# A larger planned gap between a batch's folds and its sequence products

## The chip, the cores and the metric

The kernel runs on one core of a Trainium2 chip, in fp32. Its time is the device time of one execution in microseconds (us). Five runs of the kernel before gave a median of 827.72 us (826.7 to 829.09). The names of the engines are those of the profile: PE is TensorE (matrix products), DVE is VectorE, ACT is ScalarE, POOL is GpSimd (which also issues the gathers), and SP issues most of the plain transfers.

## The reference

```python
# lightning attention: q, k, v (4, 8, 768, 64), lam (8,)
intra = einsum('bhij,bhjd->bhid', einsum('bhic,bhjc->bhij', qb, kb) * Dmask, vb)
inter = einsum('bhid,bhde->bhie', qb * lam_pow, kv_state)
out[:, :, sl] = intra + inter
kv_state = lam_block * kv_state + einsum('bhsd,bhse->bhde', kb * rev_pow, vb)
# bridge: x[b, s, h*64 + d] = out[b, h, s, d]          (4, 768, 512)
# FNet block, w_ch1 (512, 2048), w_ch2 (2048, 512)
mixed = real(fft(fft(x, axis=1), axis=2))
u = x + mixed
un = (u - mean(u)) / sqrt(var(u) + 1e-6)
result = u + maximum(un @ w_ch1, 0) @ w_ch2
```

Each of the four batches is independent of the others, apart from the weights that all share.

## The kernel before, in words

**A batch's front.** Attention goes through a batch in six chunks of 128 rows (`NC` = 6). `attn_in` loads k, q and v of a chunk (L263), turns k and q with PE (L274, L279), copies them out with ACT (`kT` L276, `qT` L281) and scales q with DVE (L285). `attn_out` makes the scores (16 products L298, which take the two halves of PE's rows in turn), multiplies them by the decay on DVE (`sc`, two of L302), updates the state (L315 on PE, L317 or L320 on DVE), adds the state's part and the scores' part (L328, L332), copies the result out (L335) and turns it (L348) into x. Parts of x go to DRAM (`xa`, `xb`; L363 to L367), since the Fourier mixing needs rows in mirrored order: POOL gathers these (`mirror_a`, L439 and L445; `mirror_b`, L452).

`fft_ln` then mixes. By the symmetry of a real Fourier transform, `fold_a` and `fold_b` first add and subtract mirrored rows and columns on DVE (L426 to L430 and L470 to L484). The sequence products (L516, against the table `cs`, in two pieces of 128 and 65 rows) and the width products (L529 to L534, against `dt`) follow. DVE combines them (L596 to L609), normalises (statistics L546 and L547, the root on POOL L550 and L551, `un` L564), and the result is kept for the MLP: of the first four groups of 256 rows it is turned with PE (L569), of the other eight it is turned in blocks by DVE (L574) and stored by SP (L578, L584).

**The MLP.** The twelve groups are named `(b, g)`. The first four, `PLAIN`, are multiplied plainly by `mlp`: for each of 16 blocks of the hidden width, four products with `w1` (L633, a "group" of four below) and a relu on ACT or DVE (L641, L639); then for each of two tiles of 128 rows, products with `w2` (L647), the addition of u (L654 and L655 in a first half, L658 and L659 in the last part, into `y`), and the store (L620 by SP, or L622, a scatter by POOL). Three of the four are done in two halves of the hidden width. The other eight, `LATE`, are done after all fronts, in pairs, with fewer block products by a Strassen-Winograd form (L720, L767). The weights come in double precision and are converted on the way by ACT and DVE (`load_weights`, L209 to L225).

**What sets the order.** The functions are generators. They issue instructions and then yield a number, the time on PE or DVE that the planner takes as due for what came since the last yield. `weave(lead, other, ratio)` runs the `lead`, and after each of its yields draws from `other` until that one's sum reaches the lead's sum times `ratio`. `beside` derives the ratio from planned lengths. A yield that follows no instruction of its own is a request for so much other work at that place. In the last two of these weaves the fronts of batches 1 (rest), 2 and 3 run against the plain products: in the first, the products lead, the fronts get `t_rest * t_half / t_back` units; in the second, the fronts lead. A further scheduler then fixes the order of instructions on each engine from the program as built, taking account of their data and of the buffers that they take over; some instructions are pinned in program order.

The lengths that concern the change: `t_chunk` = 7.3, `t_front` = 6 x 7.3 + 13.0 + 7.0 + 5.7 + 3 x 2.4 = 76.7, `t_mlp` = 54.4, `t_half` = 81.6, `t_back` = 167.6, `t_rest` = 3 x 76.7 - 5 x 7.3 = 193.6. `LEADS` = (0,), so `b - 1 in LEADS` holds for batch 1 only, and L508 gives 12.0 for batch 1 and 9.0 for batches 2 and 3. Batch 0 takes another branch.

**Buffers.** x tiles come from a pool of 12; a gathered x (L452) takes over the buffer of an older one, such as the u of a plain tile whose last reader is L659. PE's results go to five buffers (`pa`, fronts) and three (`pm`, products).

Of the kernel before, what the change touches and what calls it, by code (L numbers as in the profile page):

```python
# [76 lines left out]
def kernel(  # L77
# [15 lines left out]
    NC = S // C  # L93
# [161 lines left out]
    LEADS = (0,)  # L255
# [200 lines left out]
    def fold_a(b):  # L456
        for a, n in enumerate(BLK):
            yield from fold_x(b, a, n, 1, eo[b][a][1][0:n, 1, 0:DM], xn_[b, HC + a][0:n])

    def fold_b(b, sets):  # L460

        tt = nc.vector.tensor_tensor
        for a, n in enumerate(BLK):
            yield from fold_x(b, a, n, 0, xs[b, a][0:n], xs[b, HC + a][0:n])
            e, o = eo[b][a]
            nc.scalar.copy(e[0:n, :, HM:HM + 1], e[0:n, :, DM - 1:DM])

            am, bm = e[0:n, :, W:2 * W], o[0:n, :, W:2 * W]
            lo, hi = e[0:n, 0, 0:HM + 1], e[0:n, 1, 0:HM + 1]
            tt(am[:, 0, 0:HM + 1], lo, hi, op=ALU.add)  # L470
            tt(am[:, 1, 0:HM + 1], lo, hi, op=ALU.subtract)
            yield 0.8

            lo, hi = am[:, :, 0:QM], am[:, :, HM:QM:-1]
            tt(e[0:n, :, 0:QM], lo, hi, op=ALU.add)
            tt(e[0:n, :, QM:HM], lo, hi, op=ALU.subtract)
            yield 0.8
            lo, hi = o[0:n, 0, 1:HM], o[0:n, 1, 1:HM]
            tt(bm[:, 0, 1:HM], lo, hi, op=ALU.subtract)
            tt(bm[:, 1, 1:HM], lo, hi, op=ALU.add)  # L480
            yield 0.8
            lo, hi = bm[:, :, 1:QM + 1], bm[:, :, HM - 1:QM - 1:-1]
            tt(o[0:n, :, 0:QM], lo, hi, op=ALU.subtract)
            tt(o[0:n, :, QM:HM], lo, hi, op=ALU.add)  # L484
            yield 0.8
            sets.append((e, o))
        eo.pop(b)
# [3 lines left out]
    def fft_ln(b):  # L491
# [7 lines left out]
        if b in LEADS:  # L499
            yield from fold_a(b)  # L500
            yield from fold_b(b, sets)
            yield 2.0
        else:
            yield 1.0
            run(fold_a(b))
            yield 6.0 if b - 1 in LEADS else 3.0
            run(fold_b(b, sets))
            yield 12.0 if b - 1 in LEADS else 9.0  # L508


        for i in range(5):
# [288 lines left out]
    def front(b):  # L800
        yield from attn(b)
        yield from fft_ln(b)
# [15 lines left out]
    def run(gen):  # L818
        return sum(gen)
# [12 lines left out]
    NW = 2 * KO * DFF // WP  # L832
    w = weights()
    t_chunk = 7.3
    t_front = NC * t_chunk + 13.0 + 7.0 + 5.7 + 3 * 2.4
    t_mlp = FO * 1.7 + G * 4 * 3.4

    def beside(lead, t, other, t_other):
        return weave(lead, part(other, t_other), t_other / t)

    att1, mix = attn(1), fft_ln(0)
    att0 = attn(0)
    run(part(att0, 2.7))
# [4 lines left out]

    half = [[mlp(b, g, h * FO // 2, (h + 1) * FO // 2) for b, g in PLAIN[:3]] for h in range(2)]
    fr = chain([att1, fft_ln(1)] + [front(b) for b in range(2, B)])  # L850
    t_rest, t_back = 3 * t_front - 5 * t_chunk, len(PLAIN) * t_mlp - 50.0
    t_half = 1.5 * t_mlp
# [50 lines left out]
```

## Time and profile before

| | us |
|---|---|
| median of 5 runs | 827.72 (826.7 to 829.09) |
| the profiled execution's own time | 825.68 |
| its span | 823.9 |
| PE busy in the span | 797.0 |
| end of the fronts and plain products, start of the late pairs | about 433 |

The times of instructions come from one profiled execution, which took 825.68 us; 1.8 us of it lie around the span. The granted clock of PE was 0.996 of full speed. In lists of instructions each line has the start and the duration in us, the engine, the line of the kernel, the operation with its output and inputs, and how many instructions of a kind follow each other. A bracket at the end is the idle time of the engine ahead of the instruction, and the instruction that ended it. In fp32 each matrix product appears as two records. In lists of waits the columns are the sum in us, how many times, and the longest. [...]

### The profile page before, as it was taken

The page shows a single profiled execution, that of the slowest core. Times are in us where ns is not written, and L with a number is a line of the kernel's source. Part 1 is how long each engine was busy: PE and PEld are TensorE (multiplying, and loading weights), DVE is VectorE, ACT ScalarE, POOL GpSimd, SP SyncE. Part 2 cuts the span into 40 slices and gives each one's busy share as a digit, 9 for nine tenths or more (in the row PEclk, how much of TensorE's full clock was granted, in tenths as well). Part 3 has the DMA queues.
Part 4 walks back from the last instruction along what each step waited for, and adds up shares of the span by engine and source line. Part 5 has one row for each costly group of instructions (what it writes and reads, how often), then busy time and mean ns, then how long its engine had stood idle before and what let it go on. Part 6 is the DMA issues. An engine that isn't in the chain of part 4 may idle for free.

```text
span 823.9 us, 11701 instructions
## 1 busy us (share of the span) xinstructions
PE 797.0 (97%) x4608; PEld 636.2 (77%) x4608; DVE 437.8 (53%) x1018; ACT 186.4 (23%) x448; POOL 79.9 (10%) x102
## 2 busy tenths in 40 slices
PE   6889799999999999999999999999999999999998
PEld 5777676758585857768748888888888888888886
DVE  6899779675744571345895541155313661146311
ACT  3655343324420211222102200022001210012100
POOL 3123310011010110220100000000000000000000
PEclk9999899999999999999999999999999999999999
DMA  9969443238841137530442011100111001000010
GB/s 235 251 146 272 107 154 103 77 77 217 205 117 59 64 65 141 128 122 1 115 126 79 1 53 51 52 1 0 58 46 52 0 1 39 33 33 0 1 39 25
DMA packets 126684, 68.88 MB, mean 84 GB/s; under 512 B 111150, under 2 KB 112174, under 8 KB 126630
## 3 DMA queue, kind: packets, MB, share of 16 engines
q1 hardware_dynamic: 121488, 55.67, 26.3%
q0 software_dynamic: 2112, 6.69, 2.5%
q10 hardware_dynamic: 3030, 5.78, 1.9%
q8 instruction: 36, 0.59, 0.3%
q14 instruction: 18, 0.15, 0.1%
HBM read 48.72 MB, written 19.40 MB: 83 GB/s over the span
## 4 chain that ended last, share of the span: by engine, by line
PE 81%; DVE 10%; issue 4%; DMA 2%; ACT 2%; POOL 1%; SPq 0%; POOLq 0%; ACTq 0%; DVEq 0%
PE p L767 24%; PE p L720 23%; PE pm L647 10%; PE pm L633 8%; PE pa L298 3%; PE pa L516 3%; PE pa L332 3%; PE pa L328 2%; PE pa L274 1%; PE pa L315 1%; PE pa L348 1%; PE pa L279 1%; DVE fe L426 1%; DMA x<-xb,ix 1%; DVE fo L427 1%
## 5 line engine op out<-in xcount | busy, mean ns | idle before, releaser
L633 PE MATMUL pm<-ut,w 128*128 128x256 f32 x512 | 119.9, 383 | 0.0
L647 PE MATMUL pm<-w,hr 128*128 128x512 f32 x256 | 115.8, 597 | 0.3 <-DVE w L225 0.3
L633 PEld LDWEIGHTS pm<-ut,w 128*128 128x128 f32 x512 | 94.2, 190 | 15.8 <-issue 4.1
L720 PE MATMUL p<-ur,w 128*128 128x256 f32 x384 | 93.8, 379 | 0.0
L647 PEld LDWEIGHTS pm<-w,hr 128*128 128x128 f32 x256 | 46.7, 190 | 49.7 <-issue 47.8
L720 PEld LDWEIGHTS p<-ur,w 128*128 128x128 f32 x384 | 73.0, 190 | 10.3 <-issue 0.5
L720 PE MATMUL p<-us,w1s 128*128 128x256 f32 x256 | 65.7, 379 | 0.0
L767 PE MATMUL p<-w,hs 128*128 128x256 f32 x256 | 58.0, 379 | 0.5 <-DVE y L788 0.5
L767 PE MATMUL p<-w2s,hs 128*128 128x256 f32 x256 | 57.9, 379 | 0.0
L767 PE MATMUL p<-w,ha 128*128 128x256 f32 x256 | 57.9, 379 | 0.0
L767 PEld LDWEIGHTS p<-w,hs 128*128 128x128 f32 x256 | 48.5, 190 | 7.5 <-DVE y L788 0.9
L767 PEld LDWEIGHTS p<-w2s,hs 128*128 128x128 f32 x256 | 48.6, 190 | 6.6
L767 PEld LDWEIGHTS p<-w,ha 128*128 128x128 f32 x256 | 48.6, 190 | 6.6
L720 PEld LDWEIGHTS p<-us,w1s 128*128 128x128 f32 x256 | 48.6, 190 | 6.6
L622 POOL DMA_INDIRECT out_dram<-y,ix x12 | 11.9, 988 | 401.9 <-DVE y L793 342.3
L747 ACT COPY ha<-p 128x256 f32<-128x256 f32 x32 | 11.9, 372 | 169.1 <-PE p L720 139.4
L758 DVE TENSOR_TENSOR ha<-p,ha 128x256 f32<-128x256 f32 x32 | 13.6, 424 | 45.2 <-ACT ha L757 45.2
L298 PEld LDWEIGHTS pa<-qT,kT 64*128 64x128 f32 x384 | 26.3, 194 | 13.2 <-ACT qT L281 7.1
L302 DVE TENSOR_TENSOR sc<-pa,decay 128x512 f32<-128x512 f32 x48 | 31.5, 683 | 8.8 <-PE pa L298 8.5
L332 PE MATMUL pa<-sc,v 128*64 128x128 f32 x384 | 31.6, 281 | 3.7 <-DVE sc L302 3.5
L298 PE MATMUL pa<-qT,kT 64*128 64x128 f32 x384 | 30.9, 293 | 3.3 <-ACT qT L281 3.0
L720 PE MATMUL p<-us,w 128*128 128x256 f32 x128 | 32.9, 379 | 0.0
(144 smaller groups left out, 1122.3 us busy)
## 6 DMA issues: line engine op xcount, KB each, us to landing
raw<-in_moe_w_ch_dram SPq DMA_DIRECT2D x32, 512.0 KB, 5.0
k<-in_k_dram SPq DMA_DIRECT2D x24, 256.0 KB, 5.0
q<-in_q_dram SPq DMA_DIRECT2D x24, 256.0 KB, 5.9
v<-in_v_dram SPq DMA_DIRECT2D x24, 256.0 KB, 4.4
ud<-x SPq DMA_DIRECT2D x16, 256.0 KB, 2.3
utd<-e SPq DMA_DIRECT2D x64, 64.0 KB, 2.2
u<-ud SPq DMA_DIRECT2D x16, 256.0 KB, 2.7
ur<-utd SPq DMA_DIRECT2D x6, 512.0 KB, 4.9
```

The costliest lines, as they stand in the source:

```text
L298: mm(pss[hi][:, hp, :], lhsT=kT[HD[hi], hp, :], rhs=qT[HD[hi], hp, :], start=True, stop=True)
L302: nc.vector.tensor_tensor(t, pss[hi], decay[:, hi::2, :], op=ALU.mult)
L328: mm(po[HD[hi], hp, :], lhsT=s_old[HD[hi], hp, :], rhs=qs[HD[hi], hp, :], start=(hp == 0), stop=False, skip_group_check=True)
L332: mm(po[HD[hi], hp, :], lhsT=vt[:, 2 * hp + hi, :], rhs=sc[hi][:, hp, :], start=(c == 0 and hp == 0), stop=(hp == HP - 1), skip_group_chec ...
L516: mm = nc.tensor.matmul(ps[0:m, n, :], lhsT=piece(a, i, n), rhs=cs[0:rows, a, i in (2, 3), n, :], start=(a == 0), stop=(a == 1))
L622: nc.gpsimd.indirect_dma_start(out=out.rearrange("b s d -> (b s) d"), out_offset=row_of(2 + HC * (b + 1) + T - HC), in_=y[:, :], in_offset ...
L633: nc.tensor.matmul(ps, lhsT=w1[:, c, 128 * fc:128 * fc + 128], rhs=ut[:, c, :], start=(c == 0), stop=(c == KO - 1))
L647: nc.tensor.matmul(ps, lhsT=hr[(fc - f0) // 4][:, fc % 4, 128 * i:128 * i + 128], rhs=w2[:, fc, :], start=(fc == f0), stop=(fc == f1 - 1))
L720: nc.tensor.matmul(ps, lhsT=s2.A[a][:, kt, 128 * i:128 * i + 128], rhs=U[b][:, kt, :], start=(first and kt == 0), stop=(kt == 1), skip_gro ...
L747: nc.scalar.copy(a11, two(X))
L758: V.tensor_tensor(a22, two(Z), a22, op=ADD)
L767: nc.tensor.matmul(ps, lhsT=h[a][:, s, i, :], rhs=s2.B[b][:, i, :], start=(first and i == 0), stop=(i == HF - 1), skip_group_check=True)
```

## The change

Two constants grow by 2.5. At the end of the folds of batches 2 and 3, ahead of their sequence products, the yield becomes 11.5 in place of 9.0. The planned length of a front becomes 79.2 in place of 76.7, and through it `t_rest` 201.1 in place of 193.6. What is computed, by which instructions and from which buffers' pools, stays as it is; the order of instructions on the engines changes from batch 1's mixing on.

```diff
             yield 6.0 if b - 1 in LEADS else 3.0
             run(fold_b(b, sets))
-            yield 12.0 if b - 1 in LEADS else 9.0
+            yield 12.0 if b - 1 in LEADS else 11.5
...
-    t_front = NC * t_chunk + 13.0 + 7.0 + 5.7 + 3 * 2.4
+    t_front = NC * t_chunk + 15.5 + 7.0 + 5.7 + 3 * 2.4
```

The code that turns these numbers into an order:

```python
    def beside(lead, t, other, t_other):
        return weave(lead, part(other, t_other), t_other / t)
...
    t_rest, t_back = 3 * t_front - 5 * t_chunk, len(PLAIN) * t_mlp - 50.0
    run(beside(beside(chain(half[0]), t_half, w, 0.5 * NW), t_half + 0.5 * NW, fr, t_rest * t_half / t_back))
...
    run(weave(fr, back, (t_back - t_half) / (t_rest - t_rest * t_half / t_back)))
```

## The prediction

> **What bounds the kernel now.** I read the page's busy row first, then a table of stages, then TensorE's waits in the stage that the change touches, and last the two places where the change aims. The page:
>
> ```profile
> span 823.9 us, 11701 instructions
> PE 797.0 (97%) x4608; PEld 636.2 (77%) x4608; DVE 437.8 (53%) x1018; ACT 186.4 (23%) x448; POOL 79.9 (10%) x102
> ```
>
> TensorE (PE) is the bound: 26.9 us of the span are not its busy time. The stage table (PE busy is the first figure after the stretch's length) says where these lie:
>
> ```profile
> 0.00:134.00 134.00, 116.16 (x1062) 89.90 (x1062) 111.61 (x243) 64.94 (x146) 34.56 (x45) 0.97 0.71 183
> 134.00:433.00 299.00, 294.02 (x1757) 206.43 (x1757) 183.27 (x386) 73.38 (x174) 36.55 (x48) 1.00 0.43 110
> 433.00:823.90 390.90, 386.86 (x1792) 339.86 (x1790) 142.97 (x391) 48.05 (x128) 8.75 (x9) 1.00 0.09 29
> ```
>
> In the built order of the changed program the first stage and the last hold the same instructions in the same order as before. All that the change can win lies in the middle one: 299.00 - 294.02 = 5.0 us. TensorE's waits there (in all, times, longest):
>
> ```profile
> PE pa L516 <- DVE fe L475: 2.2, 3, 1.1
> PE pa L332 <- DVE sc L302: 1.6, 1, 1.6
> PE pa L569 <- DVE un L564: 0.9, 1, 0.9
> PE pm L647 <- DVE w L225: 0.3, 1, 0.3
> ```
>
> The first row is the change's aim: the sequence products L516 of batches 2 and 3 find their fold unfinished, 1.06 + 0.19 us in batch 2 and 0.95 in batch 3. What holds the fold, in batch 2, all engines:
>
> ```profile
> 257.50 0.41 DVE L659 TENSOR_TENSOR y<-pm,x 128x256 f32<-128x256 f32 x1
> ...
> 258.19 0.94 POOL L452 DMA_INDIRECT x<-xb,ix  x1 [11.88 <-DVE y L659]
> ...
> 261.58 0.69 DVE L426 TENSOR_TENSOR fe<-x,x 128x512 f32<-128x512 f32 x1 [3.66 <-DMA x<-xb,ix]
> ...
> 265.06 0.90 PE L516 MATMUL pa<-cs,fe 128*128 128x193 f32 x4 [1.06 <-DVE fe L475]
> ```
>
> The gather L452 doesn't wait for the attention. It waits for L659, the end of a plain MLP tile, whose x buffer it takes over. So the fold is released by the products themselves.
>
> **What the Trainium skill says.** "Perfetto Trace Analysis", Identifying the Most-Contended Engine: matmul busy time misleads, and weight-load time is to be read beside it. Here that is 77%, with PE waits nearly absent after 134 us; I judge by waits. The same page, Optimization Strategy, has one find the gaps and what would end them: done above. Its Sequencer Loop lets an instruction wait in its engine's queue for its semaphores; the trace agrees, a wait of 0.56 us at L564 standing directly ahead of a score's scaling:
>
> ```profile
> 171.07 0.74 DVE L564 TENSOR_SCALAR un<-x,mv,rs 128x256 f32<-128x256 f32 x2 [0.56 <-POOL rs L551]
> 171.72 0.68 DVE L302 TENSOR_TENSOR sc<-pa,decay 128x512 f32<-128x512 f32 x1
> ```
>
> **The change part by part.** Nothing is added or removed: each engine has the same instructions. (a) The due at L508 rises 2.5 for batches 2 and 3. (b) The planned length of a front rises 2.5, 76.7 to 79.2, and counts three times, so three fronts are planned 7.5 longer while only two are, by 5. With t_rest 193.6 to 201.1 and t_half/t_back 81.6/167.6, the first weave gives the front 97.9 for 94.3 units; the last one's products per front unit fall from 86/99.3 = 0.866 to 86/103.2 = 0.833. L508 is thus worth 9 x 0.866 = 7.79 before and 11.5 x 0.833 = 9.58 after: 1.79 product units, one L633 group more (due 1.7; 8 records, 3.62/16 x 8 = 1.8 us). Everything else in the fronts gets 4% fewer products beside it. Following the built order of both programs, with durations from the trace:
>
> Batch 2, L508. Between the last L348 and the first L516 there are 17.25 us of products before, 18.98 after. But the added group comes ahead of the MLP tile that releases the gather; from the tile's end at 257.0 to L516 stand the same 16 L647 records (6.9 us), against a chain of 8.0 (gather issue 258.19, data in use 261.58, eight fold steps on DVE). The gap 1.06 stays, and the 0.19 behind it: **0**.
>
> Batch 3, L508. After the last L348 there are 8 L647 records and 32 L633 before (3.43 + 6.91) and 12 and 24 after (5.15 + 5.19): 10.34 both times. Here the gather waits for the row's own DMA, so the chain is unmoved: the 0.95 stays. **0**.
>
> What is left is the 4%, which regroups products in the attention chunks. In fp32 each matmul is two records.
>
> - Batch 1's mixing: L569 follows 5 L633 matmuls instead of 3, but a weight step (L225, 0.6) and a relu come ahead of its un. The stall of 0.94 becomes about 1.05: **+0.1**.
> - Batch 2, chunk 0. Before, 6 L647 records, L315 and 8 L647 records (6.65 us) lie between L298 and L332; the 8 move behind L332, leaving 3.2. The second sc ends at 171.72 + 0.68 = 172.4 (queued behind L564's wait above), while PE comes to L332 at 175.30 - 3.45 = 171.85. With the 0.1 from a sc's end to its L332, a new wait of 0.65. But the width products of batch 1's last two parts now have one L633 matmul between them, not seven, so DVE gets that mixing earlier; adding up its new queue from 154.6 (with the wait for rs, 1.2 us after L547, as in the trace) I get 172.05 for the sc's end, a wait of 0.3. I take the middle: **+0.5** (0 to 1.7, if two DVE steps more come ahead).
> - Chunk 1. The 16 L298 run in turn between the two row halves, which they don't before (1.16 us for 16 elsewhere, 1.63 here): **-0.37**. L298 to L332 goes from 4.7 to 3.4 us of cover, against 2.0 of DVE work: 0.
> - Chunk 2: L332 is no longer cut by an L633 (re-entry after each switch, 0.43): **-0.43**.
> - Chunk 3. L279 to L298 falls from 3.0 to 0.87 us, while qT needs a copy of 0.59 behind another on ACT, and the row halves fall out of turn (0.37): **+0.65** (0.4 to 1.2).
> - Batch 3, chunk 0. The third wait row:
>
> ```profile
> 298.94 0.43 PE L332 MATMUL pa<-sc,v 128*64 128x128 f32 x2 [1.57 <-DVE sc L302]
> 299.31 0.55 PE L274 MATMUL pa<-ident,k 128*128 128x128 f32 x3
> ```
>
>
> L302 is late because DVE is full with batch 2's last mixing (back to back from 293.65 to 299.8). The front runs one L633 group earlier and the cover grows from 3.2 to 4.9 us; PE reaches L332 at the same time, and the second sc has moved behind five other DVE steps, to end near 299.2. The wait stays, about 1.8, but L332 isn't cut by L274: **-0.4** (-1.7, if DVE's backlog starts earlier too, to +0.3).
> - Chunks 1 to 5 of batch 3: covers change by under 2 us and stay above need; 0. The group that the front overtakes there lands in a row of products without a wait: 0.
>
> These last two are hidden by the products queued on PE; with that cover gone each would cost up to the group's 1.7. On SP's queue some weight loads change places with loads of k, q and v. The tightest of these (batch 2, chunk 3, issued at 197.83, transposed at 206.14) takes 5.0 us to land, so 3.3 are spare, and it moves ahead of a weight load: 0. POOL's gathers and scatters keep their order: 0.
>
> Sum: 0.1 + 0.5 - 0.37 - 0.43 + 0.65 - 0.4 = **+0.05 us**. The profiled execution took 825.68 (span 823.9 and 1.8 around it), 2.0 below the median of the runs, 827.72. I carry the difference over: 827.8. The ends of the terms (0, 0, -0.37, -0.43, +0.4, -1.7, and 0.2, 1.7, 0, 0, 1.2, 0.3) put this at -2.1 to +3.4; not all fall alike, so the forecast's own range is -1.2 to +1.6 us, 826.5 to 829.3.
>
> **Rivals.**
> - *The fold waits close.* If the gather's wait is set by issue time rather than by the tile, or the added group slips behind the tile, 1.06 + 0.19 + 0.95 = 2.2 us go. For it: it is what the due does by its name. Against: the releaser above, L659, and equal work in batch 3. Time 827.72 - 2.2 = 825.5; with the 1.57 as well, 823.9.
> - *DVE's queue becomes what PE waits for, in batch 2's first chunks (slower).* The place is L332 of chunk 0 and L298 of chunks 1 and 3. Between the end of L298 and the end of the second sc DVE has 4.1 us of work before (168.28 to 172.40); the cover left is 3.2. My forecast has about 4.0. Should one weight step (L224, 1.1) and one width step (L600, 0.7) come ahead of that sc too, the wait grows by 1.8; with chunk 3 at its upper end, 0.55 more: 0.05 + 1.8 + 0.55 = +2.4, 830.1. It decides (over 0.2%) from about 5.6 us of DVE work there. For it: L564's wait in this very queue. Against: the earlier width products just named.
> - *The change doesn't do what it says*: a longer due that buys no cover at all. That is in my forecast, batch 3's equal 10.34 us.
>
> **How the numbers follow.** 0.2% of 827.72 is 1.66 us, about what a measurement of this kernel tells from no change: faster is below 826.06, slower above 829.38. The forecast has 0.45, DVE's queue 0.30, the closing waits 0.25. The first lies almost all within 0.2%, the others outside. The 8-in-10 range takes in most of both: 825.6 (nearly the whole 2.2) to 830.6 (the slower rival and 0.5 more).
>
> **What would show it.** Right: the L516 rows of batches 2 and 3 keep waits of about 1.1 and 0.95 on L475; the gather before batch 2's L516 still names L659; a new wait L332 on L302 of 0.2 to 0.8 near 172; the wait at the next batch's first chunk stays at 1.5 to 2. Wrong: no L516 wait left (first rival), or waits of L332 and L298 that sum to 4 or more in the middle stage (second). It would also be wrong if the last stage changed in length: then the cause would be outside all this.

## The result, and the profile after

The kernel after took 827.79 us (median of 41 runs, 825.96 to 830.25) and the kernel before 826.47 (median of 78 runs, 824.8 to 830.64). The ratio is 1.0017, with a 95% interval of 1.0011 to 1.0024: 1.4 us slower, which is within the 0.2% named in the prediction. The five runs that the prediction started from had a higher median, 827.72. The profiled execution took 828.27 us.

The busy row of the page after:

```profile
span 826.5 us, 11699 instructions
PE 798.4 (97%) x4608; PEld 637.4 (77%) x4608; DVE 438.8 (53%) x1018; ACT 186.8 (23%) x448; POOL 79.5 (10%) x102
```

PE is still the bound. The middle row of the stage table, with the same borders as before:

```profile
134.00:433.00 299.00, 292.66 (x1754) 205.69 (x1753) 184.73 (x388) 73.69 (x175) 37.03 (x48) 1.00 0.42 110
```

In the middle stage PE is now idle for 299.00 - 292.66 = 6.3 us; it was 5.0. PE's waits there:

```profile
PE pa L516 <- DVE fe L475: 2.9, 4, 1.0
PE pa L332 <- DVE sc L302: 1.9, 2, 1.3
PE pa L569 <- DVE un L564: 0.9, 1, 0.9
PE pm L647 <- DVE w L225: 0.4, 1, 0.4
PE pm L633 <- DVE hr L639: 0.2, 1, 0.2
```

The row that the change aims at, L516, has grown from 2.2 us in three waits to 2.9 in four, the row L332 has a second wait, and there is a new row for L633. Where these are, in the list of PE's instructions:

```profile
172.48 0.43 PE L332 MATMUL pa<-sc,v 128*64 128x128 f32 x2
173.58 1.09 PE L332 MATMUL pa<-sc,v 128*64 128x128 f32 x14 [0.67 <-DVE sc L302]
...
266.22 0.90 PE L516 MATMUL pa<-cs,fe 128*128 128x193 f32 x4 [0.97 <-DVE fe L475]
...
300.35 1.09 PE L332 MATMUL pa<-sc,v 128*64 128x128 f32 x14 [1.27 <-DVE sc L302]
...
371.96 0.59 PE L516 MATMUL pa<-cs,fe 128*128 128x193 f32 x2 [0.79 <-DVE fe L475]
...
376.86 2.23 PE L516 MATMUL pa<-cs,fe 65*128 65x193 f32 x12 [0.96 <-DVE fe L475]
...
403.78 3.72 PE L633 MATMUL pm<-ut,w 128*128 128x256 f32 x16 [0.19 <-DVE hr L639]
```

Batch 2's fold wait (0.97) and batch 3's second one (0.96) are still there. New are 0.67 in batch 2's first chunk, 0.79 at batch 3's first sequence product, and 0.19 behind the front. One wait is shorter, that in batch 3's first chunk: 1.27 after 1.57.

Waits alone don't give the sum, since a row of products that is cut in two also costs. So I compared both traces at the same work: the start of the same instruction of a front in both, corrected for the plain products that have gone ahead of it in one program and not in the other (0.43 us for each L633 product of two records, 0.86 for each L647). A difference that appears between two such marks arose between them. The comparison begins at batch 1's first L516, up to which the order is the same in both programs. It stands at 135.26 us before and 136.13 after. That 0.87 us is no effect of the change.

| place | predicted | measured, us |
|---|---|---|
| batch 1's mixing, L569 | +0.1 | -0.06 |
| batch 2, chunk 0 | +0.5 | +0.91 |
| chunk 1 | -0.37 | -0.68 |
| chunk 2 | -0.43 | -0.57 |
| chunk 3, with 4 | +0.65 | +0.75 |
| batch 2's fold | 0 | -0.10 |
| batch 3, chunk 0 | -0.4 | -0.26 |
| batch 3, chunk 1 | 0 | -0.20 |
| batch 3's fold | 0 | **+0.97** |
| behind the fronts, to the late pairs | 0 | **+0.53** |
| not placed, ahead of the late pairs | | +0.07 |
| late pairs | 0 | +0.33 |
| sum from batch 1's first L516 | +0.05 | +1.69 |

The timing says +1.4 (0.9 to 2.0). Of the 1.69 in the traces, about 1.2 is idle time of PE (5.91 after 4.72 up to the late pairs), and 0.33 belongs to the last stage. The prediction's terms for the mixing and the chunks sum to 0.05; these rows measure -0.11, chunk 1 of batch 3 among them. The loss is in the two bold rows, which the prediction had at nothing.

**Batch 3's fold.** The gather of the last rows waits for the last DMA write `xb` (L367). ACT's issue of that write, and POOL's gathers, in the kernel after (ACTq is ACT's queue of issues):

```profile
361.55 0.33 ACTq L367 DMA_DIRECT2D xb<-xn  x1
```

```profile
360.26 0.99 POOL L445 DMA_INDIRECT x<-xa,ix  x1 [0.30 <-issue]
...
365.30 0.94 POOL L452 DMA_INDIRECT x<-xb,ix  x1 [4.05 <-DMA xb<-xn]
```

The same in the kernel before:

```profile
362.56 0.33 ACTq L367 DMA_DIRECT2D xb<-xn  x1
```

```profile
359.55 0.99 POOL L445 DMA_INDIRECT x<-xa,ix  x1 [0.30 <-issue]
...
365.39 0.94 POOL L452 DMA_INDIRECT x<-xb,ix  x1 [4.84 <-DMA xb<-xn]
```

The write is issued 1.0 us earlier after the change, and PE runs earlier with it, but the gather starts at nearly the same time: from issue to gather is 3.75 us in place of 2.83. What stands differently is the third gather from `xa` (L445): 3.0 us ahead of the write before, 1.3 us after. The fold isn't earlier, PE is, and this shows as the new wait of 0.79. An experiment below tests the gather as the cause.

**Behind the fronts.** The longer planned front leaves one more group of L633 products to run after the last width products. Before:

```profile
399.90 5.45 PE L633 MATMUL pm<-ut,w 128*128 128x256 f32 x24
```

These 24 records of L633 take 5.29 us up to the first L647 at 405.19. After, 32 take from 399.87 to 407.34, 7.47 us; at 0.22 us a record, 7.05 would do. The relu that PE waits for (`hr`, L639) is on DVE, behind the mixing (L600):

```profile
402.71 0.69 DVE L600 TENSOR_TENSOR x<-x,ds 128x512 f32<-128x512 f32 x1
403.31 0.42 DVE L639 TENSOR_SCALAR hr<-pm 128x256 f32<-128x256 f32 x1
```

Of the difference of 0.42, 0.19 is the bracket above and the rest a slower restart of the row; another 0.1 comes at the change to L647.

**The last stage.** The first eight records of L720 take 2.20 us after, 1.89 before; behind them both traces keep step. In the kernel after the fifth of them starts at 435.99, 0.15 us behind the end of L659 (435.84), the last step of the last plain tile. In two versions below (due of 13 for batch 3) PE waits for L659 by name at this record, and starts it the same 0.15 behind. In the kernel before, the fifth record starts at 433.52, ahead of L659's end (433.75), so it doesn't need this tile there. The +0.33 looks like a short wait for a buffer that this tile frees (0.08 us idle, and a slower restart), but the trace after doesn't name the releaser.

### The profile page after: what moved, and what is told of

Its sections match the earlier page's. It is cut to its first block, busy times and chain, and to the rows that moved or that the text cites. A ratio compares the mean times of both kernels' runs of the same rounds, so it can differ in the third digit from the quotient of the medians.

```text
span 826.5 us, 11699 instructions
## 1 busy us (share of the span) xinstructions
PE 798.4 (97%) x4608; PEld 637.4 (77%) x4608; DVE 438.8 (53%) x1018; ACT 186.8 (23%) x448; POOL 79.5 (10%) x102
## 4 chain that ended last, share of the span: by engine, by line
PE 77%; DVE 12%; issue 4%; DMA 3%; ACT 2%; POOL 1%; POOLq 0%; DVEq 0%; ACTq 0%; SPq 0%
PE p L767 23%; PE p L720 23%; PE pm L647 9%; PE pm L633 6%; PE pa L332 3%; PE pa L516 3%; PE pa L298 3%; PE pa L328 2%; DVE stt L546 1%; DMA raw<-in_moe_w_ch_dram 1%; PE pa L274 1%; DVE un L564 1%; PE pa L315 1%; PE pa L348 1%; DVE sc L302 1%
## 5 line engine op out<-in xcount | busy, mean ns | idle before, releaser
L633 PE MATMUL pm<-ut,w 128*128 128x256 f32 x512 | 120.2, 383 | 0.2 <-DVE hr L639 0.2
L647 PE MATMUL pm<-w,hr 128*128 128x512 f32 x256 | 115.5, 597 | 0.4 <-DVE w L225 0.4
L633 PEld LDWEIGHTS pm<-ut,w 128*128 128x128 f32 x512 | 94.1, 190 | 16.2 <-issue 4.1
L720 PE MATMUL p<-ur,w 128*128 128x256 f32 x384 | 94.1, 379 | 0.1
L647 PEld LDWEIGHTS pm<-w,hr 128*128 128x128 f32 x256 | 46.8, 190 | 50.8 <-issue 48.7
L720 PEld LDWEIGHTS p<-ur,w 128*128 128x128 f32 x384 | 72.9, 190 | 10.7 <-issue 0.5
L720 PE MATMUL p<-us,w1s 128*128 128x256 f32 x256 | 65.7, 379 | 0.0
L720 PEld LDWEIGHTS p<-us,w1s 128*128 128x128 f32 x256 | 48.6, 190 | 6.6
L298 PEld LDWEIGHTS pa<-qT,kT 64*128 64x128 f32 x384 | 26.8, 198 | 13.0 <-ACT qT L281 6.3
L302 DVE TENSOR_TENSOR sc<-pa,decay 128x512 f32<-128x512 f32 x48 | 31.3, 681 | 10.4 <-PE pa L298 10.2
L332 PE MATMUL pa<-sc,v 128*64 128x128 f32 x384 | 32.2, 286 | 3.4 <-DVE sc L302 3.4
L298 PE MATMUL pa<-qT,kT 64*128 64x128 f32 x384 | 31.5, 297 | 2.9 <-ACT qT L281 2.6
L720 PE MATMUL p<-us,w 128*128 128x256 f32 x128 | 32.9, 379 | 0.0
```

The lines of the kernel that those rows point to most:

```text
L298: mm(pss[hi][:, hp, :], lhsT=kT[HD[hi], hp, :], rhs=qT[HD[hi], hp, :], start=True, stop=True)
L302: nc.vector.tensor_tensor(t, pss[hi], decay[:, hi::2, :], op=ALU.mult)
L332: mm(po[HD[hi], hp, :], lhsT=vt[:, 2 * hp + hi, :], rhs=sc[hi][:, hp, :], start=(c == 0 and hp == 0), stop=(hp == HP - 1), skip_group_chec ...
L633: nc.tensor.matmul(ps, lhsT=w1[:, c, 128 * fc:128 * fc + 128], rhs=ut[:, c, :], start=(c == 0), stop=(c == KO - 1))
L647: nc.tensor.matmul(ps, lhsT=hr[(fc - f0) // 4][:, fc % 4, 128 * i:128 * i + 128], rhs=w2[:, fc, :], start=(fc == f0), stop=(fc == f1 - 1))
L720: nc.tensor.matmul(ps, lhsT=s2.A[a][:, kt, 128 * i:128 * i + 128], rhs=U[b][:, kt, :], start=(first and kt == 0), stop=(kt == 1), skip_gro ...
```

## The experiments

All compute the reference's outputs in full. This table has all of them. "From the first L516" is the time from batch 1's first L516 to the first product of the late pairs (L720), "from L720" the time from there to the span's end, each from the one profiled execution. The times are medians, and each version has the runs of the kernel before that were taken beside it. A ratio is not the quotient of the two medians; where runs scatter the two differ (due alone with `b12` later: 0.9978 by the medians; due 15 with `b12` later: 1.0062).

| kernel | time (before), us | ratio, 95% interval | from the first L516 | from L720 |
|---|---|---|---|---|
| before | | | 297.39 | 391.25 |
| after | 827.79 (826.47) | 1.0017, 1.0011 to 1.0024 | 298.75 | 391.58 |
| due alone | 826.26 (826.74) | 0.9987, 0.9974 to 1.0 | 295.77 | 393.21 |
| planned front alone | 829.45 (826.74) | 1.0032, 1.0022 to 1.0043 | 299.41 | 391.58 |
| due 15 for batch 2, 11.5 for batch 3 | 834.62 (826.74) | 1.0087, 1.0053 to 1.012 | 302.33 (low clock) | 399.39 (low clock) |
| after, third gather last | 826.89 (826.74) | 1.0009, 0.9996 to 1.0022 | 298.17 | 391.56 |
| due alone, `b12` later | 824.85 (826.71) | 0.9991, 0.9978 to 1.0005 | 294.91 | 392.17 |
| before, `b12` later | 827.28 (826.71) | 1.0004, 0.9991 to 1.0018 | 297.52 | 391.25 |
| due 15 and 11.5, `b12` later | 831.83 (826.71) | 1.0079, 1.0051 to 1.0108 | 295.65 | 397.72 (low clock) |
| due 9 for batch 2, 13 for batch 3, `b12` later | 828.36 (826.71) | 1.0033, 1.002 to 1.0046 | 297.78 | 393.68 |
| after, cover of chunk 0 back | 827.23 (826.69) | 1.0011, 0.9998 to 1.0025 | 296.82 | 391.25 |
| due alone, `b12` later, one store by POOL | 824.46 (826.69) | 0.9978, 0.9965 to 0.9992 | 295.02 | 391.35 |
| due 13 for batch 3, the same two edits | 827.47 (826.69) | 1.0011, 1.0003 to 1.0019 | 297.76 | 392.27 |
| before, the same two edits | 826.15 (827.46) | 0.9985, 0.9975 to 0.9996 | 297.74 | 390.82 |

### Each half of the change alone

My theory was that the loss is the thinner interleaving that the longer planned front brings. The rival: the longer due by itself holds back the end of the fronts.

```diff
-            yield 12.0 if b - 1 in LEADS else 9.0
+            yield 12.0 if b - 1 in LEADS else 11.5
```

> Only the due of 11.5 (L508), the planned front left at 76.7. Built order: batch 2's chunks as before; the first sequence product of batch 2 as before (its wait of 1.06 us stays); 31 plain products instead of 20 between batch 3's last turn (L348) and its first L516, so the wait there (0.95 before, 0.79 + 0.96 with the whole change) goes. Theory A, only the covers count: 0.95 gone and the cut at batch 3's first L332 (about 0.3), so about -1.2 us, ratio 0.9985, no wait of TensorE at L720. Theory B, DVE's tail is full: batch 3's mixing ends 3.4 us later, the weights' combination (L697) and L710 to L713 end up to 3 us later, and TensorE waits 1 to 3 us at the first L720 or at L633/L647 on L639: ratio 0.9995 to 1.002.

```diff
-    t_front = NC * t_chunk + 13.0 + 7.0 + 5.7 + 3 * 2.4
+    t_front = NC * t_chunk + 15.5 + 7.0 + 5.7 + 3 * 2.4
```

> Only the planned front of 79.2, the due left at 9.0. Built order equal to the whole change up to batch 2's sequence products, so the same sum there: new wait at L332 of batch 2's chunk 0 near 172 us (0.67), L298 of chunk 1 in turn, chunk 3 out of turn. In batch 3 the sequence products have 16 plain products' cover (6 of L647, 10 of L633) where the whole change has 18, so 0.9 us more of waiting at L516 there. If the planned front makes the loss: at or above the whole change, ratio 1.0017 to 1.003. If the due makes it: 0.999 to 1.0005.

Measured: the due alone is 0.13% faster (the interval just touches no change), the planned front alone 0.32% slower. 0.9987 x 1.0032 = 1.0019, against 1.0017 for both. **Up to the late pairs the two constants pull in opposite directions:** the trace is 1.6 us shorter with the due alone and 2.0 longer with the planned front alone. How much cover each gives batch 3's fold is seen in the plain products between its last L348 and its first L516: 20 before, 18 after, 31 with the due alone, 16 with the planned front alone. By the lengths above that is 10.3, 10.3, 14.6 and 9.5 us of products. PE's waits on the fold in the middle stage with the due alone:

```profile
PE pa L516 <- DVE fe L475: 1.4, 2, 1.2
```

Both waits left are batch 2's; batch 3's are gone, and so are all waits of L332 on L302 in that stage. With the planned front alone, two of PE's instructions wait longer than in either kernel:

```profile
295.92 2.84 PE L647 MATMUL pm<-w,hr 128*128 128x512 f32 x6 [1.01 <-DVE hr L639]
...
372.66 0.93 PE L516 MATMUL pa<-cs,fe 128*128 128x193 f32 x4 [1.66 <-DVE fe L475]
```

So in the whole change the planned front takes back the cover that the due asked for. The due alone gains 1.6 us up to the late pairs (295.77 against 297.39), but gives 1.96 back behind them (393.21 against 391.25), so its trace is no shorter in sum, and the gain of 0.13% rests on the timing alone. All of the 1.96 arises in the first 16 records of the late products, which wait twice:

```profile
434.78 1.10 PE L720 MATMUL p<-us,w1s 128*128 128x256 f32 x4 [0.75 <-DVE us L711]
436.60 1.10 PE L720 MATMUL p<-ur,w 128*128 128x256 f32 x4 [0.72 <-PE p L720]
```

DVE's list shows why for the first. A combination of weights for the late pairs, `b12` (L697), fills it just ahead of the sums that the first late pair needs (L710, L711):

```profile
428.69 4.62 DVE L697 TENSOR_TENSOR w<-w 128x1024 f32<-128x1024 f32 x4
433.23 0.68 DVE L710 TENSOR_TENSOR us<-ur 128x512 f32<-128x512 f32 x1
433.94 0.69 DVE L711 TENSOR_TENSOR us<-ur,us 128x512 f32<-128x512 f32 x1
```

### Is it the gathers that slow the write?

The whole change, with batch 3's third gather from `xa` put behind the two from `xb`:

```diff
-        for t in range(2, HC):
+        for t in range(2, HC if b < 3 else 2):
...
-        for t in range(2):
+        for t in range(2 if b < 3 else HC):
...
-            gather(out=u[:, :], out_offset=None, in_=xd[b][1][:, :], in_offset=row_of(2 + t))
+            gather(out=u[:, :], out_offset=None, in_=xd[b][t < 2][:, :], in_offset=row_of(2 + t))
```

> The whole change, with batch 3's third mirrored gather (L445) issued behind the two that read xb (L452) instead of ahead; TensorE's order is the same as with the whole change. If the write of xb lands late (2.9 us after issue, 2.0 before the change) because the three gathers from xa share its DMA engines, it lands in about 2.0 to 2.3, the gather L452 starts some 0.7 us earlier and the new wait of 0.79 us at batch 3's first L516 goes to 0.1 or less, 0.6 to 0.8 us faster than the whole change (1.0008 to 1.0010 of before). If the write's own latency makes it, 0.79 stays and so does the ratio of 1.0017.

ACT's issue and POOL's gather, and the sequence products on PE:

```profile
360.44 0.33 ACTq L367 DMA_DIRECT2D xb<-xn  x1
```

```profile
363.28 1.25 POOL L452 DMA_INDIRECT x<-xb,ix  x1 [4.18 <-DMA xb<-xn]
```

```profile
370.15 0.59 PE L516 MATMUL pa<-cs,fe 128*128 128x193 f32 x2
...
375.05 2.23 PE L516 MATMUL pa<-cs,fe 65*128 65x193 f32 x12 [0.96 <-DVE fe L475]
```

From the write to the gather it is 2.84 us again, as before the change, and the wait of 0.79 is gone; the 0.96 behind it stays. The traces of all the versions agree for batch 3: the delay is 2.79 to 2.91 us in the eleven where the third gather is issued 2.6 us or more ahead of the write, or behind it, and 3.75 (after), 3.71 (planned front alone) and 4.14 (cover of chunk 0 back, below) in the three where it is issued 1.3, 1.3 and 1.1 us ahead. The trace gains 0.60 us on the kernel after (689.73 against 690.33 from the first L516 to the end). By timing, 1.0009 can't be told from 1.0017. The cause of the 0.79 is shown; how much of the 0.97 it gives back in time is not.

### The prediction's claim on batch 2's fold

The prediction said that batch 2's wait doesn't move because the added group lands ahead of the tile that releases the gather. Then a due large enough to bring a group behind that tile must end the 1.06.

```diff
-            yield 12.0 if b - 1 in LEADS else 9.0
+            yield 12.0 if b - 1 in LEADS else 15.0 if b == 2 else 11.5
```

> Dues of 15.0 for batch 2 and 11.5 for batch 3, planned front 76.7. A group of L633 (1.7 us) now lies between the plain tile that releases the gather and batch 2's first L516: if the gate is the tile's end, the wait of 1.06 goes to 0 and the small one behind it (0.19) too. Batch 3's fold wait is covered as well, so all of 2.2 us at L516 is gone. Theory A (covers alone): ratio 0.997 to 0.9985. Theory B (DVE's tail): the fronts end only just ahead of the last 28 products L647, the weights' combination comes 6 to 8 us later than before against some 4 us of idle DVE time, and TensorE waits 2 to 5 us at the first L720: ratio 1.000 to 1.004.

Measured 1.0087, slower than both expectations. The new order around the first L516, in this version:

```profile
250.07 13.90 PE L647 MATMUL pm<-w,hr 128*128 128x512 f32 x32
263.80 1.89 PE L633 MATMUL pm<-ut,w 128*128 128x256 f32 x8
265.53 0.82 PE L516 MATMUL pa<-cs,fe 128*128 128x193 f32 x4
```

The kernel after has the same plain products between the last L348 and this L516, 24 records of L633 and 32 of L647, but with every L633 first:

```profile
246.17 5.35 PE L633 MATMUL pm<-ut,w 128*128 128x256 f32 x24
251.36 13.90 PE L647 MATMUL pm<-w,hr 128*128 128x512 f32 x32
```

There PE then waits 0.97, here not at all. With equal cover in sum, it is the place of the group that counts, as the claim says. But two waits further on are new:

```profile
272.87 0.81 PE L516 MATMUL pa<-cs,fe 65*1 65x193 f32 x4 [1.38 <-DVE fe L470]
...
443.39 1.10 PE L720 MATMUL p<-us,w1s 128*128 128x256 f32 x4 [3.94 <-DVE us L711]
```

The sequence products' second piece now waits 1.38, and the start of the late pairs waits 3.94 on DVE. Plain products that are used up as cover earlier are missing at the end of the fronts, where DVE's work for the late pairs needs cover too: behind the last width products 24 records of L633 and 64 of L647 are left before, here none and 56.

These waits are the smaller part of the ratio. From the first L516 to the end this trace is 13.1 us longer than that of the kernel before (701.7 against 688.6); 4.1 of it is idle time of PE, and 9.0 is longer busy time. PE was granted half the clock from 273.75 to 287.40 and from 444.42 to 451.24, where the kernel before has the full clock. All six runs show a lower granted clock, 0.984 to 0.994, against 0.992 to 0.998 for the kernel before beside them. Both stretches begin about 1 us after PE resumed from a wait (1.38 and 3.94), but waits of 1.66, 2.19 and 2.45 in other versions were followed by none, so what brought the lower clock stays open.

### Can the tail be relieved?

`b12` isn't needed by the first late products. This version makes it behind the first block of products of the first late pair, and so behind that pair's sums; `keep_in_program_order` stops the scheduler from moving it ahead again:

```diff
-                V.tensor_tensor(o[:, i:i + n // 2], x[:, i:i + n // 2], y[:, i:i + n // 2], op=op)
+                (tc.keep_in_program_order if part and o is b12 else id)(V.tensor_tensor(o[:, i:i + n // 2], x[:, i:i + n // 2], y[:, i:i + n // 2], op=op))
...
-            last = (i, X, Z)
+            last = (i, X, Z); i or j or run(cw)
...
-    run(combine_weights(1))
+    cw = combine_weights(1); run(part(cw, 2.0))
```

With the due alone (11.5):

> The due of 11.5 alone (the first of these experiments, ratio 0.9987), and in addition the two combinations of b12 (half of the four L697 on w, 2.3 us of DVE) are made after the first block of the first late pair, where nothing needs them yet; TensorE's order is that of the due alone. If DVE's full tail makes the waits at L720 (0.75 on L711 and 0.72 behind it), L711 ends 2.3 us sooner, both go, and the ratio falls by 0.0018 to about 0.997. If they come from the banks or from the loads of ur, they stay: 0.9987.

With the kernel before, as the control:

> The kernel before with the same two combinations later, as the control. TensorE has no wait at L720 there (L711 ends 2.5 us ahead of its first use), so nothing can be won: ratio 1.000, within 0.001. If the combinations in their new place hold up DVE's relus in the late pairs, up to 1.002.

With a due of 15 for batch 2 and 11.5 for batch 3:

> Dues of 15.0 and 11.5 as in the third experiment (ratio 1.0087, wait of 3.94 us at L720 on L711), with the two combinations later. DVE's tail as the cause: the wait falls by 2.3 to about 1.6 us, ratio about 1.006. Otherwise 3.9 us stay.

With 9.0 for batch 2 and 13.0 for batch 3, which gives batch 3's fold more cover and leaves batch 2 alone:

> Due 9.0 for batch 2 as before, 13.0 for batch 3, the planned front 76.7, the two combinations later. Everything up to batch 3's last turn is as before, with the waits of 1.06 and 0.19 (batch 2's fold) and 1.57 (batch 3's first L332). Nine plain products more than before have passed by the second piece's first L516... in all 25 of L633 instead of 23 ahead of it, and 24 instead of 16 ahead of the first, so the wait of 0.95 falls to 0 to 0.3; batch 3's mixing ends 3.4 us later and the later combinations give 2.3 of that back, so at most 1 us of waiting at L720. Ratio 0.999 to 1.000; if DVE's tail takes all of it, 1.0005.

In the first of these, L711 is on DVE at 429.23 and no longer at 433.94, and the 0.75 is gone. The other wait stays:

```profile
433.14 1.10 PE L720 MATMUL p<-ur,w 128*128 128x256 f32 x4 [0.67 <-PE p L720]
```

The bracket names an earlier product of PE, but the time fits another releaser: L659, the end of the last plain tile, ends at 433.04, 0.10 us ahead. The same 0.10 lies between L659's end and the second wait of the due alone (436.50 and 436.60). The ratio, 0.9991, says no more than the due alone did. On the kernel before the edit does nothing (1.0004), since `b12` wasn't in the way there: before, L711 runs at 431.19. With the due of 15 the 3.94 on L711 is gone, but PE's idle time from the first L720 to the end hardly improves, 8.6 us after 8.7; the expected gain was a miss. (The ratios, 1.0079 after 1.0087, both contain a lower clock, 0.983 to 0.993 in the six runs here.) On PE, two other waits have come in:

```profile
438.31 1.13 PE L720 MATMUL p<-us,w1s 128*128 128x256 f32 x4 [2.95 <-ACT ha L747]
...
441.01 2.05 PE L720 MATMUL p<-ur,w 128*128 128x256 f32 x4 [1.56 <-issue]
```

The due of 13 for batch 3 was a miss as well: 1.0033. Its fold wait went from 0.95 to 0.79 only, and the stretch from the first L720 to the end is 2.4 us longer (393.68 against 391.25). On PE:

```profile
377.62 1.25 PE L516 MATMUL pa<-cs,fe 65*128 65x193 f32 x6 [0.79 <-DVE fe L475]
...
436.07 1.10 PE L720 MATMUL p<-ur,w 128*128 128x256 f32 x4 [2.19 <-DVE y L659]
```

L659 is the end of the last plain tile, and L658 ahead of it waits for the single `y` buffer: DVE has

```profile
435.17 0.42 DVE L658 TENSOR_TENSOR y<-pm,x 128x256 f32<-128x256 f32 x1 [0.90 <-DMA out_dram<-y]
```

The buffer comes free with the store of the tile before (L620). That tile was complete at 424.33, but its store stands in SP's queue behind others, and the second four of these wait for a transposition on DVE, which itself stands behind 3.48 us of weights (L697):

```profile
427.66 0.70 DVE L574 STREAM_TRANSPOSE e<-un 128x512 f32<-128x512 f32 x1
```

```profile
423.08 2.60 SPq L578 DMA_DIRECT2D utd<-e  x4
428.38 2.59 SPq L578 DMA_DIRECT2D utd<-e  x4
431.01 1.10 SPq L584 DMA_DIRECT2D ud<-x  x2
432.21 0.39 SPq L620 DMA_DIRECT2D out_dram<-y  x1
```

Ten stores of the last front are ahead of it in the queue and hold it for 9 us: 6.3 us of issuing and 2.7 of waiting for L574.

### The store moved to another queue

If the queue causes that wait, the same store issued by POOL must end it.

```diff
-            nc.sync.dma_start(out[b, 128 * T:128 * T + 128, cols], y[:, cols])
+            (nc.gpsimd if (b, T) == (1, 1) else nc.sync).dma_start(out[b, 128 * T:128 * T + 128, cols], y[:, cols])
```

With the due alone and `b12` later:

> The due alone with b12 later (ratio 0.9991, wait of 0.67 left at L720), and the store of the last plain group's first tile issued by POOL instead of SP, where it stands behind the fronts' last stores L578 and L584. If that store, late in SP's queue, keeps the one y buffer and so the last L658, L659 and a bank for L720, the 0.67 goes to 0 (L658 then waits for TensorE, not for the store): ratio about 0.998. Otherwise it stays.

With the due of 13 for batch 3 and `b12` later:

> Due of 13 for batch 3 with b12 later (ratio 1.0033, wait of 2.19 at L720 on L659), and the same store by POOL. SP's queue as the cause: the 2.19 falls to 0.3 or less, ratio 1.0005 to 1.0012. Otherwise 2.19 and 1.0033 stay.

With the kernel before and `b12` later, as the control:

> The kernel before with b12 later and the y store by POOL, the control for the fastest version (0.9978, the same with the due of 11.5). If the due makes that gain and the two edits only clear the end of the fronts for it, this one is where the kernel before is: 0.9995 to 1.0005. If the two edits alone are the gain (a better order of the first late products, no wait for a bank), it is at 0.998 to 0.999 too.

In the first, POOL issues the store at once when `y` is written, and L658 starts without a wait. POOL and PE:

```profile
421.70 0.66 POOL L620 DMA_DIRECT2D out_dram<-y  x1 [12.65 <-DVE y L659]
```

```profile
432.10 5.42 PE L720 MATMUL p<-ur,w 128*128 128x256 f32 x24 [0.29 <-PE p L720]
```

The wait of 0.67 is 0.29, and the ratio is 0.9978 (0.9965 to 0.9992): this version is faster than the kernel before, and its interval lies below that of the kernel after. In the second, the wait of 2.19 fell to 1.21 and the ratio from 1.0033 to 1.0011. The queue was a cause, but not the only one; L658 now stands at 435.33 behind other steps on DVE.

The edit has a second effect that has nothing to do with this wait. In the three versions with it the span ends 3.1 us after PE's last product, in all eleven others 3.5. At the end SP waits for the transfers in nine steps, and goes from one to the next in 0.06 us once they are done. The step that waits for the very last store is the second in the other versions, with seven more behind it; here it is the ninth, and the others are over before. So 0.4 us of the 0.7 by which the first of these traces is shorter than without the edit, and of the 1.4 in the second, come from there. The control, without any change of the due, has 0.9985 (0.9975 to 0.9996). The intervals of 0.9978 and 0.9985 overlap, so the timing doesn't settle what the due adds to the two edits of the tail. The traces from the first L516 to the end say more: 686.37 with the due against 688.56 in the control, and 688.64 for the kernel before. These are single executions, and the control's 0.15% by the timing isn't in its trace.

### The cover of chunk 0 given back

The largest new wait in the chunks is batch 2's first L332. In the whole change, a larger request ahead of it:

```diff
-        yield 1.5
+        yield 4.0 if (b, c) == (2, 0) else 1.5
```

> The whole change, with the due after the scores of batch 2's chunk 0 raised from 1.5 to 4.0, so that seven products L647 (6.0 us) instead of three lie ahead of its L332. If that wait on sc (0.67, with the cut of L332 about 0.9) is a cause of the whole change's loss, it is gone, and with the row halves in turn in chunk 1 and 23 to 24 plain products ahead of batch 3's L516 (19 with the whole change) its first wait there (0.79) goes too: about 1.5 us faster than the whole change, ratio 0.9995 to 1.0005. If these two waits are not the loss, the ratio stays at 1.0017.

The row is whole again (16 records at 175.43) and doesn't wait, nor does batch 3's first L516. But PE waits at two other places:

```profile
298.16 0.43 PE L332 MATMUL pa<-sc,v 128*64 128x128 f32 x2 [0.93 <-DVE sc L302]
...
375.95 2.23 PE L516 MATMUL pa<-cs,fe 65*128 65x193 f32 x12 [2.45 <-DVE fe L475]
```

The sequence products wait 3.8 us in the middle stage in place of 2.9; the 2.45 goes with the write that took 4.14 us to its gather. The ratio, 1.0011 (0.9998 to 1.0025), can't be told from that of the kernel after. The trace is 2.26 us shorter from the first L516, 688.07 against 690.33, though PE idles as long in the middle stage as after (299.00 - 292.74 = 6.3 us); what is shorter is PE's busy time, 796.5 against 798.4 in the span. The comparison at the same work places it, against the kernel after: -1.3 us in batch 2's chunk 0, -0.7 in its later chunks, +0.2 at its fold, -0.1 in batch 3's chunks, +0.4 at batch 3's fold, -0.5 behind the fronts (24 records of L633 are left there again, not 32) and -0.3 in the last stage. The timing shows only a part of this; its 22 runs had a granted clock of 0.989 to 0.996, those of the kernel after 0.993 to 0.998. This one stays inconclusive.

## Why the prediction was right, and where it wasn't

The time and the verdict were right: 827.8 predicted, 827.79 measured, within 0.2%. But the 827.8 stood on a start of 827.72, and over more runs the kernel before has 826.47. The difference that was forecast was nothing, and the one measured is +1.4 us (0.9 to 2.0), inside the forecast's own range of -1.2 to +1.6. That the two times agree so closely is luck: the start was 1.25 us too high and the change was taken 1.3 too low. By its steps:

- *Batch 2's fold, 0*: right. The wait is 0.97 after 1.06, and the 0.19 remains. The reason, that the added group lies ahead of the tile which releases the gather, held when the due was raised to 15: with the same products in another order that wait went.
- *The chunks of batch 2*: all four with the right sign. Chunk 0 was mis-sized: +0.91 in place of +0.5. The wait itself, 0.67, has the first of the two values worked out there (0.65), not the middle that was taken, so the earlier width products that were to shorten it show no gain; and the cut of the row of L332 (two records at 172.48, fourteen at 173.58) was not in the sum. Chunks 1 and 2 gave more than said, -0.68 and -0.57, both beyond their ends, which made up for it. The reason given for chunks 1 and 3 holds: the 16 records of L298 (eight products, not sixteen) take 1.16 us after 1.63 in chunk 1, and 1.63 after 1.16 in chunk 3.
- *Batch 1's mixing, +0.1, and batch 3's chunk 0, -0.4*: -0.06 and -0.26. The first lies just outside its ends (0 to 0.2), the second inside. The wait of 1.57 became 1.27, not 1.8; the row of L332 is no longer cut by L274, as said.
- *Batch 3's fold, "the gather waits for the row's own DMA, so the chain is unmoved: the 0.95 stays. 0"*: **this step failed.** The 0.95 stayed (0.96), and beside it came 0.79; in all +0.97. Equal cover of 10.34 us was rightly counted, but the chain of work that it covers was taken as of fixed length. It holds a transfer, and the transfer took 0.9 us longer, because the write came closer behind a gather. That PE and the write were a microsecond earlier was in the built order; that the gather wasn't earlier could be seen only in the trace. With the gather moved, the 0.79 fell to 0.09.
- *"The group that the front overtakes there lands in a row of products without a wait: 0"*: **this step failed too.** +0.53: the relu that PE waits for stands on DVE behind the mixing, and PE restarts slowly. Where 24 records are left there again, in the version with chunk 0's cover given back, the trace has 0.5 less at this place.
- *The last stage*, taken as unchanged since it has the same instructions in the same order: +0.33. By the prediction's own words a change here was a sign of being wrong. Instructions and order are the same, but the fifth late record comes out behind the last plain tile's end, with 0.08 us of idle time; that it now waits for this tile's buffer is likely, not shown.
- *Rivals.* The closing of the fold waits didn't happen with the whole change. It does happen in batch 3 with the due alone, where the whole kernel measured 0.13% faster, with an interval that touches no change. The slower rival had the wrong place: the chunks of batch 2 cost +0.4 in all, not +2.4. The third, that a longer due buys no cover, is nearest to what was seen, and its reason is the other constant: 31 products with the due alone, 18 with both.

The tension between the two constants could have been had from the built orders of the two halves. The prediction followed the built order of the whole only, and so couldn't see that a gain and a loss were cancelling.

## What to carry to other kernels

In a kernel like this one, with PE busy 97% of the span, products queued as cover are a stock: what one wait gets is taken from another, so a change of the interleaving is to be summed over every place that loses products, up to the end of the region. Build each constant's effect on the order alone before adding them up, and treat the length of a chain with a DMA in it as something that the move itself can change. Before cover is moved, look at what is queued at the region's end (weights combined on DVE, stores on SP ahead of a store that frees a buffer), because that is where missing cover comes due.

## What the runs showed of the hardware that was not expected

- The same small DRAM write took 0.9 to 1.3 us longer from its issue to the gather that depends on it when another indirect gather had been issued 1.1 to 1.3 us ahead of it (3.71, 3.75 and 4.14 us) than when that gather was 2.6 us or more ahead or came later (2.79 to 2.91 in eleven traces). By the profile the write itself landed 2.9 us after its issue (kernel after) in place of 2.0 (before). The Trainium skill, "DMA: Bandwidth & Descriptors", Latency and other measured facts, has a fixed cost of about 2 us whose main part grows with the memory's load; the trace agrees in direction, but no run here shows which part of the path was loaded. Its section Issuing engines are not separate DMA queues says that transfers from different engines run on the same DMA engines and interleave: ACT's write and POOL's gather did affect each other.
- That section also says that issuing from several engines saves only the sequencer's time, usually small beside the transfer. Here it saved more, and the measurement decides. Behind ten stores on SP, a store of a finished tile was issued 7.9 us late (424.33 to 432.21), partly because four of those ahead were waiting for their own data. It held the only `y` buffer, and PE waited 2.19 us; with the same store on POOL's queue, 1.21.
- At the start of the late pairs a wait of PE costs about 0.24 us beyond its idle time. From the first L720 to the end, 2.19 of waiting made +2.43 (due 13), 0.75 + 0.72 made +1.96 (due alone), and an idle time of 0.08 made +0.33 (after).
- Moving one store to another queue shortened the end of the program by 0.4 us (3.1 in place of 3.5 us after the last product), only because the wait for the last store then came last of SP's nine.
